# Top-k attention and two expert layers on one core: another order for the last tiles' expert stages

## The chip, the core and the metric

One core of a Trainium2 chip runs the whole program once. Five engines work side by side, each through its own list of instructions in order: TensorE (PE in the rows, with its weight loads as PEld), VectorE (DVE), ScalarE (ACT), GpSimd (POOL) and SyncE (SP), which here issues most DMAs. ACT's list issues some DMAs as well. The metric is device microseconds of one execution; the median of the runs shown counts.

## The reference

```python
scores = scale * q @ k.T                    # 2 batches, 8 heads, 576 rows, head_dim 64
kth    = the 32nd largest score of a row
attn   = softmax of the scores >= kth, all others out
x      = attn @ v                           # rows regrouped: 1152 tokens x 512
p = probs / (probs.sum(-1) + 1e-9)
out = sum over 4 experts e of p[:, e] * (relu(x @ w1[e]) @ w2[e])      # 512 -> 1024 -> 512
h = max(out @ m1, out @ m2, out @ m3)                                  # 512 -> 768
result = h @ mo                                                        # 768 -> 512
```

The second layer's matrices `m1`, `m2`, `m3` and `mo` arrive in float64, all else in float32.

## The kernel before

**Tiles and stages.** The 1152 tokens are 9 tiles of 128. Attention makes one tile after another, four head pairs each (36 pairs); its top-k runs on DVE as a chain of MAX8 and MATCH_REPLACE8. The expert layer is cut in two halves of experts (indices 0 to 3 and 4 to 7 of half-experts, `HALVES`), and a tile needs both. `STAGES` lists which tiles each stage works on; stages take the two halves in turn. Stage 0 is tile 0 alone with the first half, stages 1 to 6 are [0,1], [1,2] ... [5,6], so that each tile gets its second half in one stage and its first in the next or the other way round. Stage 7 is [6,7,8], stage 8 is [7,8]. After them come three passes of the second layer (`largest`), over three tiles each.

**Units.** A stage uses 16 weight units of 128 x 1024 (512 KB): for each of 4 half-experts two of the first layer ("a") and two of the second ("b"). SP loads a unit into one of four `raw` buffers (`w_load_to`), and `w_split_to` splits it: ACT rounds it to `whi`, then POOL subtracts to get `wlo`, in two halves of 128 x 512. From the first unit of stage `LATE` = 8 on, every other unit's subtraction is one DVE instruction of 128 x 1024 instead. Five pairs `hi`, `lo` are kept.

**Split products.** x lies split in a ring of four tiles (`xring`, xh and xl). `product` makes three matmuls for one: xl by whi, xh by whi, xh by wlo. In a first layer the 128 x 128 weight block stands and the tokens of all the stage's tiles move: 256 columns for two tiles, 384 for three. In a second layer the hidden values stand, tile by tile, and 512 columns of weights move. The hidden values are split as well: ACT makes `h` (or `hh`) with the ReLU, DVE subtracts for `hl`, every fourth time POOL.

**Float32.** Stage 0 isn't split. It multiplies whole float32 weights by `xfull`, tile 0 in float32. In the trace each such matmul has two records.

**The float64 matrices.** When attention has ended, `to_float32` narrows them in 48 pieces (`wide_load`, then two ACT, three DVE and one POOL instruction, then a DMA from ACT's list back to DRAM, from where `w_load_to` fetches them for `largest`). A new piece starts every second step of the loop, so up to three are under way. A piece's result lies in half of a `pt0` or `pt1` tile: four places, taken in turn. The first instruction of a piece, on ACT, writes there, so it waits until the DMA that emptied the place has landed.

**Order.** Nothing is scheduled at run time. A loop over attention's steps writes attention's instructions, and a counter of DVE time (`clock`) decides how many pieces of products are written in between. Each engine's list is fixed by that.

Of the kernel before, what the change touches and what calls it, by code (L numbers as in the profile page):

```python
# [27 lines left out]
WAITING = 2  # L28
S1 = 4
PAUSE = 0.8  # L30
LATE = 8
ON_POOL = ((0, 1, 2, 3, 4, 5, 6, 7), (0, 1, 2, 4, 5, 6))
W_AHEAD = 4
WIDE, W_FROM, W_STEP = 4, 306, 2
# [22 lines left out]
def kernel(  # L57
# [36 lines left out]
    def place(t):  # L94
        return (t - 1) % RING

    STAGES = [[0]] + [[t - 1, t] for t in range(1, NTILE - 2)] + [[NTILE - 3, NTILE - 2, NTILE - 1], [NTILE - 2, NTILE - 1]]
    STAGES = [sorted(x, key=place) for x in STAGES]
    HALVES = [range(E) if not n % 2 else range(E, 2 * E) for n in range(len(STAGES))]
    FIRST_IN = {t: min(n for n, x in enumerate(STAGES) if t in x) for t in range(NTILE)}  # L100
    LAST_IN = {t: max(n for n, x in enumerate(STAGES) if t in x) for t in range(NTILE)}
    assert all(set(x for n in range(len(STAGES)) if t in STAGES[n] for x in HALVES[n]) == set(range(2 * E)) for t in range(NTILE))
# [29 lines left out]
    def bank(name):  # L132
        return pg.tile([P, 512], F32, tag="g", name=name)
# [57 lines left out]
    order = list(w_units())  # L191
    w_index = {key: i for i, (key, _) in enumerate(order)}
    w_raw, w_hl = {}, {}
    w_pos = {"load": 0, "split": 0}

    def w_load_to(n):
        while w_pos["load"] < min(n, len(order)):
            key, src = order[w_pos["load"]]
            if key[1] in "cd" and narrowed[0] < WIDE * (narrow_at[key[2:]] + 1):
                return  # L200
            raw = wp.tile([P, 1024], F32, tag="raw", bufs=4, name="raw")
            nc.sync.dma_start(out=raw, in_=src)
            w_raw[key] = raw
            w_pos["load"] += 1
# [9 lines left out]
    def to_float32(n):  # L214

        raw = wide_raw.pop(n).rearrange("p (n t) -> p n t", t=2)
        low, high = raw[:, :, 0], raw[:, :, 1]
        last, hf = low.bitcast(I32), high.bitcast(F32)  # L220
        if not n % 2:
            narrow_to[0] = at.tile([P, NR, P], F32, tag="pt%d" % (n // 2 % 2), bufs=1, name="narrow").rearrange("p r n -> p (r n)")
        out = narrow_to[0][:, n % 2 * 256:n % 2 * 256 + 1024 // WIDE]
        t = out.bitcast(U32)
        nc.scalar.activation(out=out, in_=hf, func=AF.Abs)  # L225
        nc.scalar.activation(out=last, in_=low, func=AF.Copy, scale=2.0 ** -29)
        yield True
        nc.vector.scalar_tensor_tensor(out=hf, in0=out, scalar=LEAST, in1=hf, op0=ALU.is_ge, op1=ALU.mult)  # L228
        dve(1024 // WIDE)
        nc.vector.tensor_scalar(out=t, in0=high, scalar1=3, scalar2=0x3FFFFFF8, op0=ALU.logical_shift_left, op1=ALU.bitwise_and)  # L230
        dve(512 // WIDE)
        nc.vector.scalar_tensor_tensor(out=t, in0=high, scalar=0xC0000000, in1=t, op0=ALU.bitwise_and, op1=ALU.bitwise_or)  # L232
        dve(1024 // WIDE)
        yield True
        nc.gpsimd.tensor_tensor(out=out.bitcast(I32), in0=out.bitcast(I32), in1=last, op=ALU.add)  # L235
        yield True
        yield True
        wide_load(n + AHEAD_S)
        yield True
        nc.scalar.dma_start(out=narrow[wide[n // WIDE][0]][:, n % WIDE * 1024 // WIDE:(n % WIDE + 1) * 1024 // WIDE], in_=out)  # L240
        narrowed[0] = n + 1

    def w_split_to(n):
        while w_pos["split"] < min(n, len(order)):
            w_load_to(w_pos["split"] + 1)
            if w_pos["load"] == w_pos["split"]:
                return
            key, src = order[w_pos["split"]]
            raw = w_raw.pop(key)
            hi = wp.tile([P, 1024], F32R, tag="hi", name="whi")  # L250
            lo = wp.tile([P, 1024], F32R, tag="lo", name="wlo")
            nc.scalar.activation(out=hi, in_=raw, func=AF.Copy)  # L252

            late = w_pos["split"] - w_index[LATE, "a", HALVES[LATE][0], 0]
            on = nc.vector if late >= 0 and late % 2 else nc.gpsimd

            for x in (slice(0, 512), slice(512, 1024)) if on is nc.gpsimd else (slice(0, 1024),):
                on.tensor_tensor(out=lo[:, x], in0=raw[:, x], in1=hi[:, x].bitcast(F32), op=ALU.subtract)  # L258
            f = 512 if key[1] in "bd" else 256
            w_hl[key] = (hi.rearrange("p (a f) -> p a f", f=f), lo.rearrange("p (a f) -> p a f", f=f))  # L260
            w_pos["split"] += 1
            w_load_to(w_pos["split"] + 3)
# [107 lines left out]
    class Pair:  # L370
# [139 lines left out]

        def norm(self):
            assert "r" in self.did
            self.xt = xfull[:, self.hp, :] if not self.t else at.tile([P, P], F32, tag="xt", bufs=2 + WAITING, name="xt")
            nc.vector.tensor_tensor(out=self.xt, in0=self.x[:, 0:P], in1=self.r, op=ALU.mult)

        def split_x(self):
# [241 lines left out]
    def experts():  # L758
        begin = {}

        def half1(c, i, u):
            tiles = STAGES[c]
            N = len(tiles) * P
            for groups in layer1(weight((c, "a", i, u)), xs_of(tiles), N, begin.pop((c, i, u), None)):
                if groups is None:
                    tick()
                    yield True
            hh, hl = hidden(N)
            count = made_h[0] = made_h[0] + 1
            if ON_POOL_H and not count % ON_POOL_H:  # L770
                raw = ms.tile([P, 2 * WIDTH], F32, tag="tm", bufs=2, name="raw")
                later(lambda: [nc.scalar.activation(out=raw[:, g], in_=ps, func=AF.Relu) for g, ps in groups],
                      lambda: [nc.scalar.activation(out=hh[:, 0:2 * N], in_=raw[:, 0:2 * N], func=AF.Copy),  # L773
                               nc.gpsimd.tensor_tensor(out=hl[:, 0:2 * N], in0=raw[:, 0:2 * N], in1=hh[:, 0:2 * N].bitcast(F32), op=ALU.subtract),  # L774
                               made.add(("h", c, i, u))])
                yield hh, hl
                return
            dve(2 * N)
            later(lambda: [nc.scalar.activation(out=hh[:, g], in_=ps, func=AF.Relu) for g, ps in groups],
                  *[lambda: None] * H_LAG,  # L780
                  lambda: [nc.vector.scalar_tensor_tensor(out=hl[:, g], in0=ps, scalar=0.0, in1=hh[:, g].bitcast(F32),
                                                          op0=ALU.max, op1=ALU.subtract) for g, ps in groups]
                  + [made.add(("h", c, i, u))])
            yield hh, hl
# [3 lines left out]
        def half2(c, i, hs, ti):  # L788
# [2 lines left out]
                outs[t] = po.tile([P, DM], F32, tag="o", name="ps2") if ti < 2 else bank("ps2")  # L791
            ps = outs[t]
            assert {("h", c, i, 0), ("h", c, i, 1)} <= made
            yield from layer2(ps, [weight((c, "b", i, u), (c, "b", i, 0)) for u in range(2)], hs, len(STAGES[c]) * P, ti, not i % 2, i % 2 == 1)
            if not i % 2:
                return
            first = t not in accs
# [220 lines left out]
```

## Time and profile before

| | |
|---|---|
| times of three runs, us | 810.56, 812.18, 815.03 (median 812.18) |
| the profiled execution | 809.75 us, of it 808.0 us from the first to the last instruction |
| mean granted TensorE clock | 0.975 |
| PE busy | 746.8 us (92%) |
| DVE busy | 635.0 us (79%) |
| POOL busy | 552.7 us (68%) |
| ACT busy | 496.3 us (61%) |
| moved by DMA | 130.16 MB, 161 GB/s |

"Busy" is the time in which an engine's instructions run. PE's matmuls overlap, so 92% isn't the share of its peak: how much work a stretch holds is read from the distances between the starts of equal matmuls. The shares are means over very different stages.

### The profile page before, as it was taken

The page shows a single profiled execution, that of the slowest core. Times are in us where ns is not written, and L with a number is a line of the kernel's source. Part 1 is how long each engine was busy: PE and PEld are TensorE (multiplying, and loading weights), DVE is VectorE, ACT ScalarE, POOL GpSimd, SP SyncE. Part 2 cuts the span into 40 slices and gives each one's busy share as a digit, 9 for nine tenths or more (in the row PEclk, how much of TensorE's full clock was granted, in tenths as well). Part 3 has the DMA queues.
Part 4 walks back from the last instruction along what each step waited for, and adds up shares of the span by engine and source line. Part 5 has one row for each costly group of instructions (what it writes and reads, how often), then busy time and mean ns, then how long its engine had stood idle before and what let it go on. Part 6 is the DMA issues. An engine that isn't in the chain of part 4 may idle for free. (4 is left out here: it accounts for less than half of the span.)

```text
span 808.0 us, 13853 instructions
## 1 busy us (share of the span) xinstructions
PE 746.8 (92%) x4758; PEld 656.2 (81%) x4758; DVE 635.0 (79%) x1172; ACT 496.3 (61%) x1098; POOL 552.7 (68%) x467
## 2 busy tenths in 40 slices
PE   6879999999789999999999989889798689999998
PEld 3558688898679898898888978778687589899996
DVE  6999999988698989999999968977889754243341
ACT  4656868696677788788788755545446533433431
POOL 2648869887876787787868879987778653163420
PEclk9978999999899999999999999999989999999999
DMA  7663535635445444534543557776778553262511
GB/s 224 183 171 116 171 123 163 174 110 172 144 142 151 135 149 132 170 119 141 166 138 113 178 183 233 233 235 202 232 238 259 203 170 130 67 213 76 186 60 39
DMA packets 56054, 130.16 MB, mean 161 GB/s; under 512 B 9712, under 2 KB 23024, under 8 KB 55984
## 3 DMA queue, kind: packets, MB, share of 16 engines
q1 hardware_dynamic: 47632, 120.56, 48.0%
q10 hardware_dynamic: 8352, 8.72, 3.1%
q8 instruction: 37, 0.61, 0.3%
q14 instruction: 33, 0.27, 0.1%
HBM read 120.60 MB, written 8.65 MB: 160 GB/s over the span
## 5 line engine op out<-in xcount | busy, mean ns | idle before, releaser
L258 POOL TENSOR_TENSOR wlo<-raw,whi 128x512 fp32r<-128x512 f32 x274 | 367.2, 1369 | 134.8 <-ACT whi L252 134.7
L252 ACT ACTIVATE whi<-raw 128x1024 fp32r<-128x1024 f32 x164 | 169.5, 1058 | 33.3 <-POOL narrow L235 8.7
L649 PE MATMUL ps<-xl,whi 128*128 128x256 f32 (+1 forms) x584 | 174.0, 298 | 7.5 <-ACT pt L465 5.7
L650 PE MATMUL ps<-xh,whi 128*128 128x256 f32 (+1 forms) x584 | 171.8, 294 | 0.0
L651 PE MATMUL ps<-xh,wlo 128*128 128x256 f32 (+1 forms) x584 | 171.8, 294 | 0.0
L416 DVE MAX8 m<-work 128x8 f32<-128x576 f32 x216 | 154.8, 744 | 0.1
L649 PEld LDWEIGHTS ps<-xl,whi 128*128 128x128 f32 x584 | 110.8, 190 | 10.4 <-ACT pt L465 7.0
L650 PEld LDWEIGHTS ps<-xh,whi 128*128 128x128 f32 x584 | 110.8, 190 | 1.0
L651 PEld LDWEIGHTS ps<-xh,wlo 128*128 128x128 f32 x584 | 110.8, 190 | 0.0
L418 DVE MATCH_REPLACE8 work<-m,work 128x576 f32<-128x576 f32 x144 | 106.7, 741 | 0.0
L649 PE MATMUL ps<-wlo,h 128*128 128x512 f32 x224 | 91.0, 406 | 6.2 <-ACT h L773 3.3
L651 PE MATMUL ps<-whi,h 128*128 128x512 f32 x224 | 88.8, 396 | 5.8 <-POOL h L774 5.8
L650 PE MATMUL ps<-whi,h 128*128 128x512 f32 x224 | 88.6, 395 | 0.0
L258 DVE TENSOR_TENSOR wlo<-raw,whi 128x1024 fp32r<-128x1024 f32 x27 | 41.2, 1525 | 57.2 <-ACT whi L252 45.9
L225 ACT ACTIVATE narrow<-raw 128x256 f32<-128x256 f32 x48 | 20.8, 433 | 69.9 <-DMA narrow<-narrow 58.3
L235 POOL TENSOR_TENSOR narrow<-narrow,raw 128x256 int32<-128x256 int32 x48 | 44.3, 926 | 24.0 <-DVE narrow L232 8.3
L403 ACT ACTIVATE s<-pss 128x288 f32<-128x288 f32 x144 | 51.6, 408 | 14.4 <-PE pss L391 14.3
L651 PEld LDWEIGHTS ps<-whi,h 128*128 128x128 f32 x224 | 42.6, 190 | 17.0 <-POOL h L774 7.6
L416 DVE MAX8 m<-s 128x8 f32<-128x576 f32 x72 | 54.1, 751 | 2.8 <-ACT s L403 2.4
L649 PEld LDWEIGHTS ps<-wlo,h 128*128 128x128 f32 x224 | 42.8, 191 | 16.3 <-POOL wlo L258 5.5
L462 PE MATMUL psp<-ident,p 128*128 128x128 f32 x288 | 46.5, 287 | 9.6 <-POOL p L448 5.6
L649 PE MATMUL ps<-x2l,whi 128*128 128x384 f32 x144 | 49.4, 343 | 4.8 <-DVE x2l L853 4.8
(111 smaller groups left out, 1637.4 us busy)
## 6 DMA issues: line engine op xcount, KB each, us to landing
raw<-in_w_dram SPq DMA_DIRECT2D x128, 512.0 KB, 3.8
raw<-narrow SPq DMA_DIRECT2D x36, 512.0 KB, 3.3
raw<-in_m_dram SPq DMA_DIRECT2D x36, 256.0 KB, 4.0
whole<-in_w_dram SPq DMA_DIRECT2D x16, 512.0 KB, 5.9
narrow<-narrow ACTq DMA_DIRECT2D x48, 128.0 KB, 4.1
kraw<-in_k_dram SPq DMA_DIRECT2D x16, 288.0 KB, 4.5
qraw<-in_q_dram SPq DMA_DIRECT2D x48, 64.0 KB, 3.7
raw<-in_mo_dram SPq DMA_DIRECT2D x12, 256.0 KB, 4.7
```

What stands on the lines that cost most here:

```text
L225: nc.scalar.activation(out=out, in_=hf, func=AF.Abs)
L235: nc.gpsimd.tensor_tensor(out=out.bitcast(I32), in0=out.bitcast(I32), in1=last, op=ALU.add)
L252: nc.scalar.activation(out=hi, in_=raw, func=AF.Copy)
L258: on.tensor_tensor(out=lo[:, x], in0=raw[:, x], in1=hi[:, x].bitcast(F32), op=ALU.subtract)
L403: nc.scalar.activation(out=s[:, h, :], in_=halves[h][:, 0:SH], func=AF.Copy)
L416: nc.vector.max(m[:, 8 * r:8 * r + 8], src)
L418: nc.vector.match_replace(out=self.w[j], in_to_replace=m[:, 8 * r:8 * r + 8], in_values=src, imm_value=NEG)
L462: nc.tensor.transpose(ps[:, r * P:(r + 1) * P], self.p[:, part, part * TAIL + r * P:part * TAIL + (r + 1) * P], ident)
L649: nc.tensor.matmul(ps, lhsT=lh, rhs=rl, start=first, stop=False)
L650: nc.tensor.matmul(ps, lhsT=lh, rhs=rh, start=False, stop=False)
L651: nc.tensor.matmul(ps, lhsT=ll, rhs=rh, start=False, stop=last)
```

## The change

The stages become [0], [0,1], [1,2], [2,3], [3,4], [4,5], [5], [6,7,8], [6,7,8]. Stage 6, tile 5 with the first half of the experts, is computed in float32 as stage 0 is: `norm` writes tile 5's x to `xfull`, its 16 units aren't split but multiplied from `raw`, and no hidden value is split. Since those units keep their `raw` buffer until PE has used them, `w_load_to` gets a bound so that no load runs more than four units beyond the first one unused. Tile 6 moves from stage 6 to stage 8, which now has three tiles like stage 7. `LATE` goes from 8 to 7, so in stage 7 every other unit is subtracted on DVE, too. Converted pieces get eight places: even pieces take an `s1` tile (four of them, attention's before), odd ones take the four halves of `pt0` and `pt1`.

```diff
-LATE = 8
+LATE = 7
...
-    STAGES = [[0]] + [[t - 1, t] for t in range(1, NTILE - 2)] + [[NTILE - 3, NTILE - 2, NTILE - 1], [NTILE - 2, NTILE - 1]]
+    STAGES = [[0]] + [[t - 1, t] for t in range(1, NTILE - 3)] + [[NTILE - 4]] + [[NTILE - 3, NTILE - 2, NTILE - 1]] * 2
...
+    WHOLE = [n for n, x in enumerate(STAGES) if len(x) == 1]
...
+    whole_at = [i for i, (key, _) in enumerate(order) if key[0] in WHOLE and key[1] in "ab"]
...
+    used = [0]
+
     def w_load_to(n):
-        while w_pos["load"] < min(n, len(order)):
+        whole = [x for x in whole_at if x >= used[0]]
+        while w_pos["load"] < min(n, len(order), *[x + 4 for x in whole[:1]]):
...
         if not n % 2:
-            narrow_to[0] = at.tile([P, NR, P], F32, tag="pt%d" % (n // 2 % 2), bufs=1, name="narrow").rearrange("p r n -> p (r n)")
-        out = narrow_to[0][:, n % 2 * 256:n % 2 * 256 + 1024 // WIDE]
+            out = at.tile([P, 1024 // WIDE], F32, tag="s1", bufs=S1, name="narrow")
+        else:
+            if n % 4 == 1:
+                narrow_to[0] = at.tile([P, NR, P], F32, tag="pt%d" % (n // 4 % 2), bufs=1, name="narrow").rearrange("p r n -> p (r n)")
+            out = narrow_to[0][:, n // 2 % 2 * 256:n // 2 % 2 * 256 + 1024 // WIDE]
...
+            if key[0] in WHOLE and key[1] in "ab":
+                w_hl[key] = raw
+                w_pos["split"] += 1
+                w_load_to(w_pos["split"] + 3)
+                continue
...
-            self.xt = xfull[:, self.hp, :] if not self.t else at.tile([P, P], F32, tag="xt", bufs=2 + WAITING, name="xt")
+            self.xt = xfull[:, self.hp, :] if [self.t] in STAGES else at.tile([P, P], F32, tag="xt", bufs=2 + WAITING, name="xt")
...
+            if c in WHOLE:
+                ps = bank("ps1")
+                w = weight((c, "a", i, u)).rearrange("p (a f) -> p a f", f=256)
+                for f in range(2):
+                    for a in range(KT):
+                        pe(4 * P)
+                        nc.tensor.matmul(ps[:, f * P:(f + 1) * P], lhsT=w[:, a, f * P:(f + 1) * P], rhs=xfull[:, a, :], start=f == a == 0, stop=f == 1 and a == KT - 1)
+                    yield True
+                used[0] = w_index[c, "a", i, u] + 1
+                h = hp_.tile([P, 2, 512], F32, tag="h", bufs=4, name="hfull")[:, 0, 0:2 * P]
+                later(lambda: [nc.scalar.activation(out=h, in_=ps[:, 0:2 * P], func=AF.Relu), made.add(("h", c, i, u))])
+                yield h
+                return
...
-            yield from layer2(ps, [weight((c, "b", i, u), (c, "b", i, 0)) for u in range(2)], hs, len(STAGES[c]) * P, ti, not i % 2, i % 2 == 1)
+            if c in WHOLE:
+                for u in range(2):
+                    w = weight((c, "b", i, u), (c, "b", i, 0)).rearrange("p (f n) -> p f n", f=2)
+                    for f in range(2):
+                        pe(4 * DM)
+                        nc.tensor.matmul(ps, lhsT=hs[u][:, f * P:(f + 1) * P], rhs=w[:, f, :], start=not i % 2 and u == f == 0, stop=i % 2 == 1 and u == f == 1)
+                        yield True
+                used[0] = w_index[c, "b", i, 1] + 1
+            else:
+                yield from layer2(ps, [weight((c, "b", i, u), (c, "b", i, 0)) for u in range(2)], hs, len(STAGES[c]) * P, ti, not i % 2, i % 2 == 1)
```

What this does to the lists is seen in three places. The first is PE's list where stage 6 begins, behind the last matmuls of a second layer of stage 5. Before, with two tiles and split weights:

```order
L649 MATMUL ps_5753<-wlo,h 128x512
L650 MATMUL ps_5753<-whi,h 128x512
L651 MATMUL ps_5753<-whi,h 128x512
L649 MATMUL ps_5821<-xl,whi 128x256
L650 MATMUL ps_5821<-xh,whi 128x256
L651 MATMUL ps_5821<-xh,wlo 128x256
```

In the changed kernel, at the same place:

```order
L662 MATMUL ps_5737<-wlo,h 128x512
L663 MATMUL ps_5737<-whi,h 128x512
L664 MATMUL ps_5737<-whi,h 128x512
L783 MATMUL ps_5791<-xfull,raw 128x128 x8
L475 MATMUL psp<-ident,p 128x128 x4
L409 MATMUL pss<-kT,ql 128x288
```

A weight block's three matmuls of 256 columns have become one of 128 columns that reads the `raw` buffer itself.

The second place is SP's list around the first loads of float64 pieces (in_m_dram). Weight units are in_w_dram. Before:

```order
L304 DMA qraw<-in_q_dram 64x2x128 x2
L202 DMA raw<-in_w_dram 128x1024 x13
L212 DMA raw_6208<-in_m_dram 128x512
L212 DMA raw_6210<-in_m_dram 128x512
L212 DMA raw_6212<-in_m_dram 128x512
L212 DMA raw_6214<-in_m_dram 128x512
L212 DMA raw_6216<-in_m_dram 128x512
L202 DMA raw<-in_w_dram 128x1024 x2
L212 DMA raw_6272<-in_m_dram 128x512
```

In the changed kernel:

```order
L317 DMA qraw<-in_q_dram 64x2x128 x2
L207 DMA raw<-in_w_dram 128x1024 x10
L217 DMA raw_6082<-in_m_dram 128x512
L217 DMA raw_6084<-in_m_dram 128x512
L217 DMA raw_6086<-in_m_dram 128x512
L217 DMA raw_6088<-in_m_dram 128x512
L217 DMA raw_6090<-in_m_dram 128x512
L207 DMA raw<-in_w_dram 128x1024 x4
L217 DMA raw_6137<-in_m_dram 128x512
L217 DMA raw_6150<-in_m_dram 128x512
L207 DMA raw<-in_w_dram 128x1024 x3
```

Three unit loads fewer stand ahead of the five piece loads, and the four behind them belong to stage 6, which is then at its middle.

The third place is DVE's list where stage 7 begins, in the changed kernel (three instructions are one piece's):

```order
L728 SCALAR_TENSOR_TENSOR acc<-ps_6004,gate,acc 128x512
L271 TENSOR_TENSOR wlo<-raw,whi 128x1024
L236 SCALAR_TENSOR_TENSOR raw_6090<-narrow,raw_6090 128x256
L238 TENSOR_SCALAR narrow<-raw_6090 128x256
L240 SCALAR_TENSOR_TENSOR narrow<-raw_6090,narrow 128x256
L236 SCALAR_TENSOR_TENSOR raw_6137<-narrow,raw_6137 128x256
L238 TENSOR_SCALAR narrow<-raw_6137 128x256
```

Before, DVE's list holds pieces and hidden values there, and no weight unit:

```order
L715 SCALAR_TENSOR_TENSOR acc<-ps_6141,gate,acc 128x512
L228 SCALAR_TENSOR_TENSOR raw_6272<-narrow,raw_6272 128x256
L230 TENSOR_SCALAR narrow<-raw_6272 128x256
L232 SCALAR_TENSOR_TENSOR narrow<-raw_6272,narrow 128x256
L228 SCALAR_TENSOR_TENSOR raw_6332<-narrow,raw_6332 128x256
```

A unit's subtraction has come in between, ahead of the pieces that follow it in DVE's order.

## Rows read from the trace of the kernel before

**Rows 1.** The page: busy us of each engine, share of the span, instructions.

```profile
PE 746.8 (92%) x4758; PEld 656.2 (81%) x4758; DVE 635.0 (79%) x1172; ACT 496.3 (61%) x1098; POOL 552.7 (68%) x467
```

**Rows 2.** Busy time by stretches: length, then each engine (instructions), PE clock, DMA.

```profile
375.10:438.80 63.70, 62.67 (x470) 56.72 (x469) 60.81 (x130) 52.06 (x123) 50.41 (x44) 1.00 0.44 136
438.80:497.67 58.87, 54.80 (x381) 47.95 (x380) 50.08 (x82) 38.82 (x82) 49.79 (x42) 1.00 0.59 189
497.67:572.48 74.81, 67.00 (x325) 58.66 (x324) 61.32 (x76) 37.85 (x75) 64.67 (x56) 0.98 0.72 221
572.48:643.90 71.42, 60.79 (x337) 51.03 (x335) 58.73 (x78) 40.84 (x78) 50.71 (x39) 0.93 0.72 231
648.90:808.00 159.10, 155.49 (x834) 147.66 (x834) 55.96 (x73) 54.42 (x76) 54.96 (x38) 0.99 0.34 116
```

**Rows 3.** PE in order of time, where stages 7, 8 and the second layer begin.

```profile
497.67 0.34 PE L649 MATMUL ps<-xl,whi 128*128 128x384 f32 x1
...
498.71 0.34 PE L649 MATMUL ps<-xl,whi 128*128 128x384 f32 x1
...
569.68 0.40 PE L649 MATMUL ps<-wlo,hh 128*128 128x512 f32 x1
...
571.78 0.39 PE L649 MATMUL ps<-wlo,hh 128*128 128x512 f32 x1
...
572.48 0.28 PE L649 MATMUL ps<-xl,whi 128*128 128x256 f32 x1
...
573.90 0.28 PE L649 MATMUL ps<-xl,whi 128*128 128x256 f32 x1
...
648.90 0.52 PE L649 MATMUL ps<-x2l,whi 128*128 128x384 f32 x1 [4.79 <-DVE x2l L853]
```

**Rows 4.** PE in order of time in stage 0: float32, two records a matmul.

```profile
77.43 3.74 PE L733 MATMUL psa<-xfull,whole 128*128 128x128 f32 x32
...
87.47 2.74 PE L748 MATMUL ps<-whole,hfull 128*128 128x512 f32 x6
...
90.57 0.59 PE L748 MATMUL ps<-whole,hfull 128*128 128x512 f32 x1
```

**Rows 5.** What PE waited for between 497.67 and 643.9: us, times, longest.

```profile
PE ps L651 <- POOL h L774: 4.5, 3, 2.7
PE ps L651 <- POOL hl L774: 4.1, 2, 2.6
PE ps L649 <- POOL wlo L258: 3.5, 5, 1.2
PE ps L649 <- ACT h L773: 3.3, 1, 3.3
```

**Rows 6.** What ACT waited for in the same stretch.

```profile
ACT narrow L225 <- DMA narrow<-narrow: 54.4, 15, 7.7
ACT whi L252 <- POOL narrow L235: 8.7, 5, 2.2
```

**Rows 7.** Groups of instructions in the same stretch: busy us, mean ns, idle before.

```profile
L258 POOL TENSOR_TENSOR wlo<-raw,whi 128x512 fp32r<-128x512 f32 x51 | 72.7, 1450 | 7.2 <-ACT whi L252 7.2
...
L258 DVE TENSOR_TENSOR wlo<-raw,whi 128x1024 fp32r<-128x1024 f32 x10 | 16.3, 1633 | 4.9 <-ACT whi L252 4.9
```

**Rows 8.** A piece's instructions in the same stretch: ns least/median/most.

```profile
L230 DVE TENSOR_SCALAR narrow<-raw x39: 293/720/1721, 496.6 to 643.8; 128x256 uint32<-128x256 uint32 x39
...
L232 DVE SCALAR_TENSOR_TENSOR narrow<-raw,narrow x38: 424/851/1409, 497.9 to 636.6; 128x256 uint32<-128x256 uint32 x38
L228 DVE SCALAR_TENSOR_TENSOR raw<-narrow,raw x38: 407/828/1519, 499.8 to 642.2; 128x256 f32<-128x256 f32 x38
```

**Rows 9.** Loads from 438.8 to 497.67: KB each, median us to landing.

```profile
raw<-in_w_dram SPq DMA_DIRECT2D x14, 512.0 KB, 3.7
```

**Rows 10.** Loads from 30 to 70, around stage 0.

```profile
whole<-in_w_dram SPq DMA_DIRECT2D x8, 512.0 KB, 6.2
...
kraw<-in_k_dram SPq DMA_DIRECT2D x2, 288.0 KB, 7.6
```

## The prediction, made before the changed kernel had run

> **What bounds the kernel now.** I began with the page's busy times [rows 1]: PE is busy 92% of the span, the others 61 to 79%. That says PE counts most, not where it loses time. The stretches say that [rows 2]. In stage 5 (375.1 to 438.8) PE is busy for 62.67 of 63.70 us while DVE is at 60.81: attention and products fit together, and hardly anything is lost. In the second layer, from 648.90 on, PE is busy for 155.49 of 159.10. Between them lie stages 7 and 8 (497.67 to 643.9), where PE is busy for 67.00 of 74.81 and 60.79 of 71.42 and its clock falls to 0.98 and 0.93 on average. Attention is over there, and the float64 pieces are narrowed beside the products.
>
> How much is lost in those 146.2 us? PE's work is counted by the distance of starts [rows 3]. With 384 columns six matmuls take 498.71 − 497.67 = 1.04 us, so a weight block (three of them) takes 0.52. With 256 columns twelve take 1.42, so a block takes 0.355. In a second layer nine take 2.10, so three take 0.70. Stage 7 has 64 blocks of 0.52 (33.3) and 3 tiles x 16 x 0.70 (33.6). Stage 8 has 64 of 0.355 (22.7) and 2 x 16 x 0.70 (22.4). The last quarter of stage 6's second layer also stands there, 8 x 0.70 (5.6). Together 117.6, so **28.6 us** are not work. Named waits hold 15.4 of them, and each has ACT or POOL before it: hidden values and `wlo` that came late [rows 5]. The lower clock withholds up to 74.8 x 0.02 + 71.4 x 0.07 = 6.5.
>
> Why do ACT and POOL come late? ACT's waits answer it [rows 6]: 54.4 us in 15 waits of a piece's first instruction for the DMA that empties its place, and 8.7 behind POOL's part of a piece. ACT is busy for 37.85 + 40.84 = 78.7 [rows 2], so with these waits its list is full for 141.8 of the 146.2 us. Behind such a wait stand the ReLUs and the `whi` of the next unit; POOL's `wlo` waits for those, and PE for both.
>
> **The change part by part.** *Products.* In stage 0, float32 records start (3.74 − 0.28) / 31 = 0.112 us apart in the first layer, the tail of the last one taken like the 0.28 of a split record of 256 columns, and (2.74 − 0.59) / 5 = 0.43 in the second [rows 3, 4]. With two records a matmul, a block takes 0.223 in the first layer and 0.86 in the second. Stage 6's first layer becomes 64 x (0.223 − 0.355) = −8.4; stage 8's, now with three tiles, 64 x (0.52 − 0.355) = +10.6. In the second layer tile 5 costs 16 x (0.86 − 0.70) = +2.6, and tile 6 only moves. Sum **+4.7**, which PE pays in full, since nothing hides work on the engine that is busiest.
>
> *Eight places.* A place comes round every eighth piece in place of every fourth, and pieces start two steps apart, so the DMA that emptied it was issued seven steps earlier or more, not one. The 54.4 us of ACT's waits should nearly all go. What PE gets back is at most the 28.6, at least nothing, if another wait takes over. Next in line is DVE. From 497.67 to 643.9 it is busy for 61.32 + 58.73 = 120.1 [rows 2]. The third tile of stage 8 adds a little, and `LATE` = 7 adds eight subtractions of 1.63 in stage 7 [rows 7], some 13: about 133. PE's work from the start of stage 7 to the second layer will be 2 x (33.3 + 33.6) and 4 x 0.86 of stage 6's end, 137.2. The two are nearly level.
>
> DVE's own times can shrink. A piece's three instructions take 0.72 + 0.85 + 0.83 = 2.40 by their medians, but 0.29 + 0.42 + 0.41 = 1.12 at the least [rows 8]. POOL, busy for 64.67 + 50.71 = 115.4 us here [rows 2], does 51 half subtractions of 1.45 [rows 7]; 32 are left in the changed kernel, 27.6 us less. DVE at 133 keeps the waits, DVE at 133 − 39 x 1.28 = 83 has room. I take off a quarter of the difference, as POOL loses a quarter of its work: about 120 beside 137. On the Trainium skill, "GPSIMD Engine Reference", section Specifications: its SBUF interface is shared with VectorE, and contention arises with DVE instructions in a two-port mode or with two SBUF inputs. The spread from 293 to 1721 ns of one instruction is what this would look like. Taken alone the rule would let the pieces fall to their least times only with POOL idle, and put the eight subtractions moved to DVE into the same contention; by the least times the sum would be that of the first rival below, by the medians that of the second.
>
> So I let PE keep 11 of the 28.6 us, 8% of 137. Stage 5 shows that a DVE at 95% can leave PE less idle than that [rows 2], but a piece crosses ACT, DVE, POOL and ACT's list again, and any of these in-order lists can hold hidden values behind it. **−17.6**, bounds 0 and −28.6. The wait of 4.79 for x2l at the join to the second layer [rows 3] stays: it follows from the last tile's sum.
>
> *Stage 6 unsplit.* 16 x ACT and 32 x POOL instructions go. Much of that lies before 470 us, where PE and DVE set the pace together, so I count nothing for it, but it gave PE a cushion: five split pairs besides the four `raw` buffers. Now a buffer is loaded again only when PE has used it. A unit lasts PE 8 x 0.223 = 1.8 or 2 x 0.86 = 1.7 us, so from the release of a buffer to its next turn lie three units, 5.2 us. Loads land in 3.7 us around there [rows 9], and then nothing waits. The dense loads around stage 0 took 6.2 [rows 10], 1.0 more than the cushion, and 7.6 is the longest median there. With 16 units, four rounds, that is 0, 4 or 10 us. Stage 6 asks for 512 KB each 1.75 us beside the pieces, which is dense, so I take **+4**. While attention's matmuls still stand between, the cushion is longer. The two units of stage 7 that follow also have ACT and POOL to pass, which this has to cover.
>
> *Bookkeeping.* The bound in `w_load_to` is no instruction. Writing x to `xfull` in place of `xt` costs the same. Even pieces' `s1` tiles are free when attention is over, which is when pieces begin; if one were not, ACT would wait once for the last mask.
>
> Sum against the profiled span: 808.0 + 4.7 − 17.6 + 4 = 799.1, 8.9 less. From its 809.75 that gives 800.9. The median of the runs shown lies 2.4 above that execution, 812.18, so I predict 812.18 − 8.9 = **803**.
>
> **The rivals.** *More comes back.* DVE's times shrink toward their least, PE keeps 3 us as in a dense stage, and loads land in time: 808.0 + 4.7 − 25.6 = 787.1, so 791 by the median. For it: stage 5's packing. Against it: pieces cross four lists.
>
> *The wait changes its name.* ACT no longer waits for the DMA, but POOL's and DVE's parts of a piece are as late, DVE goes toward 133 of 137 and hidden values wait behind four pieces in its list. PE keeps 26: 808.0 + 4.7 − 2.6 + 4 = 814.1, so 818. For it: the 8.7 us that ACT already waits behind POOL's part [rows 6], and the order of DVE's list. Against it: POOL's quarter less. It decides from about 16 us kept besides the loads' 4 on: there the gain falls under 0.5%.
>
> *Slower: SP's list is held.* SP issues in order, and behind the five piece loads stand four unit loads of stage 6, behind the next two piece loads three, then one and four. Each piece load waits until POOL has finished an earlier piece. If three such holds last as long as the longest wait in a piece's chain, 7.7 us [rows 6], PE stands for 23 in stage 6: 808.0 + 4.7 − 17.6 + 23 = 818.1, so 822. It turns into a loss where holds pass (17.6 − 4.7) / 3 = 4.3 us. Against it: five pieces may be loaded ahead, and POOL has nothing to split then. On the Trainium skill, "DMA: Bandwidth & Descriptors", section "Issuing engines are not separate DMA queues": DMAs of all engines interleave on the same 16. By it, pieces that leave ACT's list sooner lengthen the landing of these very loads; the rise from 3.7 to 6.2 us agrees with such crowding, and no run here shows yet how far it goes.
>
> **How the numbers follow.** The forecast (797 to 809) gets 0.55, the first rival 0.17, the second 0.18, the third 0.10. About 0.5%, 4.1 us, is what a measurement can tell from no change: under 808.1 is faster, over 816.2 slower. Faster: 0.17 and 0.50 of the forecast's 0.55, 0.67. The second rival's values straddle the upper limit, so half of it is slower; with 0.08 of the third, slower is 0.17. The rest, 0.16, is the same. The range goes from 789, just below the first rival, to 818, the second, and leaves out mainly the third and the outer ends.
>
> **What would show it.** In the profile after: ACT's waits for DMA under a piece's first instruction nearly gone; stage 7's start to the second layer's about 148 us; its clock above 0.95. Stage 6's matmuls should have waits for in_w_dram of a few us in all. DVE in stages 7 and 8 near 120 to 125, its piece instructions with lower medians. I am wrong if ACT's waits go and PE's excess stays (then DVE or POOL releases it), if PE waits over 10 us for `raw` in stage 6, or if the last pieces arrive after stage 8 and hold the second layer's first units.

## The result, and the profile after

The changed kernel takes 790.1 us (median of four runs, 788.45 to 792.18) beside 811.37 for the kernel before in the same comparison: a ratio of 0.974, 95% interval 0.969 to 0.979. In two later comparisons it stood at 789.7 and 789.6 beside 809.7 and 809.9. The forecast was 803, range 789 to 818: the median lies 1.1 us inside the range's lower end. The profiled execution took 792.18 us, with a span of 790.3, 17.7 less than before. It is the slowest of the four, and the one of before was faster than its median, so the profiles show a little less than the medians. They are compared with each other below.

The page's line of busy times answers to [rows 1]:

```profile
PE 744.1 (94%) x4678; PEld 650.6 (82%) x4678; DVE 617.7 (78%) x1179; ACT 483.3 (61%) x1088; POOL 491.1 (62%) x419
```

PE has nearly the same busy time in a shorter span; POOL has lost 62 us. Where the span got shorter is seen from the stretches, cut at the same places as [rows 2]: stage 5, stage 6, stage 7, stage 8, second layer.

```profile
375.60:439.36 63.76, 62.73 (x469) 56.84 (x468) 61.13 (x132) 50.78 (x121) 45.49 (x40) 1.00 0.42 125
439.36:482.70 43.34, 39.72 (x270) 30.88 (x268) 29.19 (x63) 21.30 (x59) 11.22 (x12) 1.00 0.64 225
482.70:553.40 70.70, 65.23 (x310) 55.65 (x310) 56.07 (x80) 38.78 (x79) 45.12 (x37) 0.98 0.76 244
553.40:632.84 79.44, 77.36 (x385) 68.05 (x384) 74.50 (x109) 46.08 (x91) 59.23 (x48) 1.00 0.74 237
632.84:790.30 157.46, 153.87 (x835) 146.04 (x833) 53.65 (x68) 55.40 (x77) 52.17 (x37) 1.00 0.35 119
```

Stage 6 takes 43.34 us in place of 58.87, **15.5 less**. Stages 7 and 8 with the join take 150.14 in place of 151.23, **1.1 less**. The second layer takes 157.46 in place of 159.10, **1.6 less**. By the prediction's block times stage 6 has lost 8.4 + 12 x (1.40 − 0.86) = 14.9 us of work and stages 7 and 8 have gained 137.2 − 117.6 = 19.6. So stage 6 got shorter by its work and 0.6 us more, and stages 7 and 8 took in 19.6 us of work without getting longer. Their idle time, the join's 4.8 us included, fell from 33.6 to 12.9.

What PE and ACT waited for from 482.70 to 632.84 answers to [rows 5, 6] (us, times, longest):

```profile
PE ps L662 <- POOL wlo L271: 3.5, 1, 3.5
PE ps L664 <- POOL hl L800: 2.0, 2, 1.2
PE ps L664 <- POOL wlo L271: 1.6, 2, 0.8
```

```profile
ACT narrow L233 <- POOL narrow L243: 17.0, 10, 3.3
ACT whi L265 <- DMA raw<-in_w_dram: 11.7, 4, 5.3
ACT whi L265 <- POOL narrow L243: 11.2, 6, 3.0
```

The 54.4 us behind a piece's DMA are gone. In their place ACT stands 28 us behind POOL's part of a piece, which its list's DMAs wait for, and 11.7 for weight units, hardly there before (0.3 us).

A piece's DVE instructions in that stretch, beside [rows 8]:

```profile
L236 DVE SCALAR_TENSOR_TENSOR raw<-narrow,raw x44: 410/421/1039, 486.3 to 622.6; 128x256 f32<-128x256 f32 x44
L238 DVE TENSOR_SCALAR narrow<-raw x44: 293/725/1844, 487.3 to 623.1; 128x256 uint32<-128x256 uint32 x44
L240 DVE SCALAR_TENSOR_TENSOR narrow<-raw,narrow x44: 424/426/1495, 487.6 to 623.8; 128x256 uint32<-128x256 uint32 x44
```

Two of three medians are halved. By the means a piece's three instructions fell less, from 2.41 us together to 2.00, and 44 pieces lie in the stretch in place of 39. POOL is busy for 104 us there and not 115. The last piece's last DVE instruction starts at 623.8, nine us ahead of the join.

PE in order of time, stage 6 and the start of stage 7, then the join, answers to [rows 3, 4]:

```profile
465.97 3.74 PE L783 MATMUL ps<-xfull,raw 128*128 128x128 f32 x32
469.54 3.60 PE L825 MATMUL ps<-raw,hfull 128*128 128x512 f32 x8
...
475.74 2.05 PE L783 MATMUL ps<-xfull,raw 128*128 128x128 f32 x16 [0.82 <-DMA raw<-in_w_dram]
479.13 3.67 PE L825 MATMUL ps<-raw,hfull 128*128 128x512 f32 x8 [1.34 <-DMA raw<-in_w_dram]
...
484.09 0.44 PE L664 MATMUL ps<-xh,wlo 128*128 128x384 f32 x1 [0.79 <-POOL wlo L271]
...
632.84 0.34 PE L662 MATMUL ps<-x2l,whi 128*128 128x384 f32 x1
633.02 0.34 PE L663 MATMUL ps<-x2h,whi 128*128 128x384 f32 x1
```

The float32 rows have exactly stage 0's length (3.74 for 32 records; (3.60 − 0.59) / 7 = 0.43). Stage 6 waits for loads twice, 2.2 us in all, and stage 7 begins with a late `wlo`. The join has no wait. Stage 6's unit loads, from 439.4 to 482.7, beside [rows 9] with 3.7 us:

```profile
raw<-in_w_dram SPq DMA_DIRECT2D x14, 512.0 KB, 5.4
```

### The profile page after: what moved, and what is told of

Read it like the earlier page. It is cut to its first block, busy times and chain, and to the rows that moved or that the text cites. A ratio compares the mean times of both kernels' runs of the same rounds, so it can differ in the third digit from the quotient of the medians.

```text
span 790.3 us, 13610 instructions
## 1 busy us (share of the span) xinstructions
PE 744.1 (94%) x4678; PEld 650.6 (82%) x4678; DVE 617.7 (78%) x1179; ACT 483.3 (61%) x1088; POOL 491.1 (62%) x419
## 4 chain that ended last, share of the span: by engine, by line
PE 55%; POOL 9%; issue 7%; DVE 6%; ACT 5%; DMA 3%; ACTq 0%; SPq 0%; POOLq 0%; DVEq 0%
PE ps L662 13%; PE ps L664 13%; PE ps L663 13%; POOL wlo L271 6%; PE psv L520 3%; DMA raw<-in_w_dram 3%; PE pss L409 2%; ACT whi L265 2%; PE pso L664 2%; PE pso L663 2%; PE pso L662 2%; PE psp L475 2%; DVE m L429 1%; PE ps L783 1%; POOL narrow L243 1%
## 5 line engine op out<-in xcount | busy, mean ns | idle before, releaser
L271 POOL TENSOR_TENSOR wlo<-raw,whi 128x512 fp32r<-128x512 f32 x228 | 302.5, 1356 | 151.9 <-ACT whi L265 151.6
L265 ACT ACTIVATE whi<-raw 128x1024 fp32r<-128x1024 f32 x148 | 153.6, 1060 | 60.8 <-DMA raw<-in_w_dram 24.5
L662 PE MATMUL ps<-xl,whi 128*128 128x256 f32 (+1 forms) x520 | 159.5, 307 | 5.5 <-ACT pt L478 5.1
L664 PE MATMUL ps<-xh,wlo 128*128 128x256 f32 (+1 forms) x520 | 157.9, 304 | 1.6 <-POOL wlo L271 1.6
L663 PE MATMUL ps<-xh,whi 128*128 128x256 f32 (+1 forms) x520 | 157.6, 303 | 0.0
L662 PE MATMUL ps<-wlo,h 128*128 128x512 f32 x160 | 64.5, 403 | 0.6 <-POOL wlo L271 0.6
L664 PE MATMUL ps<-whi,h 128*128 128x512 f32 x160 | 62.8, 392 | 0.5 <-POOL h L800 0.5
L663 PE MATMUL ps<-whi,h 128*128 128x512 f32 x160 | 63.1, 394 | 0.0
L431 DVE MATCH_REPLACE8 work<-m,s 128x576 f32<-128x576 f32 x72 | 53.2, 739 | 0.0
L475 PEld LDWEIGHTS psp<-ident,p 128*128 128x128 f32 x288 | 35.2, 146 | 19.1 <-POOL p L461 6.9
L664 PE MATMUL ps<-x2h,wlo 128*128 128x384 f32 x144 | 48.7, 338 | 0.0
```

The source lines that it names most:

```text
L431: nc.vector.match_replace(out=self.w[j], in_to_replace=m[:, 8 * r:8 * r + 8], in_values=src, imm_value=NEG)
L475: nc.tensor.transpose(ps[:, r * P:(r + 1) * P], self.p[:, part, part * TAIL + r * P:part * TAIL + (r + 1) * P], ident)
L662: nc.tensor.matmul(ps, lhsT=lh, rhs=rl, start=first, stop=False)
L663: nc.tensor.matmul(ps, lhsT=lh, rhs=rh, start=False, stop=False)
L664: nc.tensor.matmul(ps, lhsT=ll, rhs=rh, start=False, stop=last)
```

## The experiments

At first I held that the eight places had given nearly all: ACT's waits are what they remove. The rival was the new order of stages with the unsplit stage 6. The first four kernels take the change apart.

**Eight places alone.** The kernel before, with this part of the diff only:

```diff
-            narrow_to[0] = at.tile([P, NR, P], F32, tag="pt%d" % (n // 2 % 2), bufs=1, name="narrow").rearrange("p r n -> p (r n)")
-        out = narrow_to[0][:, n % 2 * 256:n % 2 * 256 + 1024 // WIDE]
+            out = at.tile([P, 1024 // WIDE], F32, tag="s1", bufs=S1, name="narrow")
+        else:
+            if n % 4 == 1:
+                narrow_to[0] = at.tile([P, NR, P], F32, tag="pt%d" % (n // 4 % 2), bufs=1, name="narrow").rearrange("p r n -> p (r n)")
+            out = narrow_to[0][:, n // 2 % 2 * 256:n // 2 % 2 * 256 + 1024 // WIDE]
```

> The kernel before with eight places for converted pieces and nothing else. Theory (ACT standing for the DMA of a piece is what idles PE in stages 7 and 8 and at the join to the second layer): ACT's 54.4 us of waits for that DMA fall under 5, the stretch from stage 7's start to the second layer falls from 151 to 125 to 133 us, the join's 4.8 us go, and the time falls by 18 to 25 us against the kernel before, as far as or a little further than the whole change. Rival (the places matter only with the relief that the unsplit stage 6 gives POOL and ACT): the waits go, but POOL or DVE takes over and the time falls by under 9 us.

Measured: 797.6 beside 809.7 us, ratio 0.985 (0.983 to 0.988), 12 us less. The stretches, from stage 6 to the second layer (the same columns as above), and what PE and ACT waited for in the second and third:

```profile
439.30:498.20 58.90, 54.77 (x381) 47.93 (x380) 52.47 (x83) 39.80 (x84) 49.92 (x42) 1.00 0.61 190
498.20:570.60 72.40, 66.64 (x325) 58.94 (x325) 67.45 (x78) 39.01 (x77) 65.25 (x56) 0.98 0.77 235
570.60:639.20 68.60, 56.45 (x338) 48.03 (x336) 66.12 (x84) 41.23 (x77) 55.08 (x43) 0.98 0.78 252
```

```profile
PE ps L652 <- DVE x2l L856: 6.2, 1, 6.2
PE ps L654 <- POOL h L777: 4.8, 3, 2.7
```

```profile
ACT whi L255 <- POOL narrow L238: 13.4, 6, 5.7
ACT narrow L228 <- POOL narrow L238: 12.7, 7, 2.9
```

No wait for a piece's DMA is left, and still stages 7 and 8 take 141.0 us for 117.6 of work. DVE is busy for 67.45 + 66.12 = 133.6 of them, POOL for 120.3. The wait has changed its name, and neither theory's numbers fit: more than 9 us came, but not 18.

**Four places in the changed kernel**, the same edit the other way:

> The changed kernel with four places for converted pieces as before. Theory: the waits of ACT for the DMA come back (40 to 60 us) and with them PE's idle time; the time is 15 to 25 us above the changed kernel, thus -3 to +5 us against the kernel before (the 4.7 us of more PE work are then paid for nothing). Rival (relief by the unsplit stage and the new order make the gain): 3 to 9 us above the changed kernel, still 10 or more below the kernel before.

Measured: 796.6 beside 809.7 us, 0.985 (0.981 to 0.988), 13 us less than before and some 7 more than the changed kernel. ACT waits again:

```profile
ACT narrow L230 <- DMA narrow<-narrow: 48.3, 17, 7.2
```

```profile
436.70:479.70 43.00, 39.76 (x270) 30.88 (x268) 29.24 (x63) 21.29 (x59) 11.16 (x12) 1.00 0.65 227
479.70:550.40 70.70, 65.45 (x309) 54.17 (x309) 52.33 (x80) 37.02 (x75) 43.99 (x37) 1.00 0.75 242
550.40:634.70 84.30, 77.98 (x385) 67.95 (x384) 73.95 (x109) 47.15 (x95) 57.94 (x48) 1.00 0.71 223
```

My theory falls here. With ACT's waits nearly as long as ever, stages 7 and 8 take 155.0 us, 3.8 more than before, though they hold 19.6 more of PE's work, and stage 6 is 15.9 shorter. PE had been idle there for 33.6 us, and the work that the new order moves in fills that time. Without the eight places, the new order with float32 in stage 6 and `LATE` = 7 gives 13 us; the places alone give 12, and all together 20 to 21, less than the sum. I read that as both drawing on the same idle time. What the order gives without float32 and `LATE` = 7 is looked at further below.

**LATE = 8 in the changed kernel:**

> The changed kernel with LATE = 8, so that stage 7's subtractions are all on POOL again. Theory (PE bounds, neither DVE nor POOL is near its limit once ACT is free): within 3 us of the changed kernel; POOL busy in stage 7 rises by about 20 us, DVE falls by about 13. Rival one (DVE is next to PE): 3 us or more faster. Rival two (POOL is next): 5 us or more slower, with waits of PE for wlo.

Measured: 792.2 us, 0.979 (0.976 to 0.981), within noise of the changed kernel, as the theory had it. Its numbers for the engines didn't come: in the 150.6 us from stage 7's start to the second layer, DVE did 10 subtractions in place of 17 and was busy for more, 137.14 us beside 130.6, and POOL for 118.40. The 44 pieces take it: by the means, a piece's three DVE instructions took 2.41 us and not 2.00.

```profile
481.90:632.50 150.60, 143.18 (x693) 123.82 (x693) 137.14 (x181) 84.92 (x170) 118.40 (x99) 0.99 0.75 239
```

**Stage 6 split**, in the changed kernel:

```diff
-    WHOLE = [n for n, x in enumerate(STAGES) if len(x) == 1]
+    WHOLE = []
```

> The changed kernel with stage 6 (tile 5 alone) computed with split weights and split x as other stages are. Theory (leaving the split out is what makes a stage of one tile possible, because 16 units of 2.7 us on POOL don't fit beside one tile's matmuls): PE's work falls in the second layer by 16 x 0.16 = 2.6 us, but stage 6 grows from 43 to 48 us or more with PE waiting for wlo, and the time is 3 to 12 us above the changed kernel. Rival (only PE's work counts): 0 to 5 us below the changed kernel.

Measured: 788.1 beside 809.7 us, 0.973 (0.971 to 0.976). The theory falls: the split stage isn't held by POOL, and leaving the split out gained nothing. The stretches are stage 6, then 7 and 8. Below them, three of its matmuls of 128 columns follow each other in stage 6.

```profile
437.20:484.30 47.10, 45.03 (x345) 40.04 (x344) 32.19 (x65) 33.58 (x71) 41.16 (x36) 1.00 0.59 184
484.30:627.40 143.10, 138.98 (x697) 123.61 (x696) 137.16 (x189) 85.06 (x171) 105.51 (x86) 1.00 0.81 255
```

```profile
463.77 0.28 PE L663 MATMUL ps<-xh,whi 128*128 128x128 f32 x1
463.88 0.27 PE L664 MATMUL ps<-xh,wlo 128*128 128x128 f32 x1
463.99 0.28 PE L662 MATMUL ps<-xl,whi 128*128 128x128 f32 x1
```

A split matmul of 128 columns starts each 0.11 us, hardly faster than one of 256 (0.118), so a block costs 0.333 beside 0.223 in float32. Stage 6 thus has 64 x 0.11 = 7.0 more and 16 x 0.16 = 2.6 less work, part of it in stage 7. But stages 7 and 8 take 143.1 for 136.6 of work: 6.5 idle, not 12.9. What they don't have is the changed kernel's start of stage 7. Its waits of ACT from 478 to 515:

```profile
ACT whi L265 <- DMA raw<-in_w_dram: 21.2, 4, 10.4
```

With stage 6 split, the same waits from 480 to 517 come to 5.9 us. SP's list in the changed kernel, and what it waited for from 439.36 to 515, show why the units of stage 7 come late:

```profile
477.83 0.33 SPq L207 DMA_DIRECT2D raw<-in_w_dram  x1
487.01 0.33 SPq L217 DMA_DIRECT2D raw<-in_m_dram  x1
487.44 2.07 SPq L207 DMA_DIRECT2D raw<-in_w_dram  x4
```

```profile
SPq L207 <- PE ps L783: 19.8, 6, 8.7
SPq L217 <- POOL narrow L243: 16.5, 4, 8.8
```

The load at 477.83 had to wait until PE had used an unsplit unit. ACT's `whi` of the unit starts at 481.57, POOL's `wlo` follows, and behind it in POOL's list stands a part of a piece, which ends at 486.98. The piece load at 487.01 waits for that part, and four unit loads stand behind it in SP's list. So one late unit makes the next ones late. In all, float32 gives PE some 4.4 us of work less and takes back about as much in late units.

**Pieces without their work on DVE and POOL.** To see which of the two limits, ACT's DMA waits or the engines' work, binds at which point, these leave out a piece's three DVE instructions and the one on POOL; the lists stay in order otherwise. The first is the kernel before, the second the kernel before with eight places.

```diff
-        nc.vector.scalar_tensor_tensor(out=hf, in0=out, scalar=LEAST, in1=hf, op0=ALU.is_ge, op1=ALU.mult)
...
-        nc.vector.tensor_scalar(out=t, in0=high, scalar1=3, scalar2=0x3FFFFFF8, op0=ALU.logical_shift_left, op1=ALU.bitwise_and)
...
-        nc.vector.scalar_tensor_tensor(out=t, in0=high, scalar=0xC0000000, in1=t, op0=ALU.bitwise_and, op1=ALU.bitwise_or)
...
-        nc.gpsimd.tensor_tensor(out=out.bitcast(I32), in0=out.bitcast(I32), in1=last, op=ALU.add)
```

> The kernel before, four places, but a piece has only its two ACT instructions and its DMAs: the three DVE instructions and the one on POOL are left out, so the narrowed values are not those of the reference. Theory (ACT standing for the DMA binds stages 7 and 8 there): ACT's waits for the DMA of a piece stay over 30 us and the stretch from stage 7's start to the second layer, 151 us, falls only to 130 to 142. Rival (the work of the pieces on DVE and POOL binds): it falls to 118 to 128, near PE's 117.6.

> The kernel before with eight places and the same cheap pieces (DVE and POOL parts left out). With eight places and whole pieces the stretch took 140.9 us with DVE busy for 133.7 of it. Theory (with the DMA waits gone DVE and POOL bound the stretch, so the eight places alone could give back only ten of its 33.6 idle us): it falls to 118 to 124, PE's 117.6 and little more. Rival (something else, loads of units or the join, holds PE): it stays over 132.

Measured: 781.6 and 772.0 beside 809.7 us, 0.968 (0.964 to 0.972) and 0.953 (0.951 to 0.956). From stage 7's start to the second layer, with four places and its longest wait of ACT, then with eight:

```profile
496.20:630.70 134.50, 124.24 (x661) 108.79 (x660) 33.74 (x43) 77.99 (x153) 78.40 (x56) 0.96 0.76 246
```

```profile
ACT narrow L225 <- DMA narrow<-narrow: 51.3, 15, 8.1
```

```profile
494.30:612.80 118.50, 118.39 (x661) 106.50 (x659) 31.99 (x42) 77.30 (x149) 69.19 (x54) 1.00 0.84 277
```

In the profiles both expectations held: with DVE nearly free, ACT's waits for the DMA stay with four places, and the stretch is 16 us longer than with eight. But the profiled execution with four places is the slowest of its four, 789.95 us, 8.4 above the median. By the medians four places cost 9.6 us, so in a median execution the stretch may well have been under 130, where the rival had it; this wasn't measured. With eight, PE is busy for 118.39 of 118.50 us, and the block times' 117.6 are confirmed to a per cent. The four stretches are 151.2 us before, 141.0 with eight places, 134.5 with cheap pieces, 118.5 with both. By the medians of the whole kernel, eight places give 12.1 us with whole pieces and 9.6 with cheap ones, and cheap pieces 28.1 with four places and 25.6 with eight. So two causes hold PE up, each shown by taking it away, and their costs nearly add. Which of DVE and POOL makes the second isn't separated here, since cheap pieces relieve both.

**One step later for a piece's DMA**, in the kernel with stage 6 split and in the changed kernel:

```diff
+        yield True
         nc.scalar.dma_start(out=narrow[wide[n // WIDE][0]][:, n % WIDE * 1024 // WIDE:(n % WIDE + 1) * 1024 // WIDE], in_=out)
```

> The changed kernel once more, so that the split stage 6 and the next kernels stand beside it on one chip: 20 to 22 us below the kernel before.

> The changed kernel with stage 6 split, and with each piece's DMA issued one step later in ACT's list (eight places leave room for it). Theory (what ACT still waits for, 24.6 us behind POOL's part of a piece, stands in front of that DMA and delays the next unit's whi): these waits fall to under 12 us, PE's idle time in stages 7 and 8 falls by 1 to 4 us, and the time is 1 to 5 us below the kernel with stage 6 split. Rival (DVE, busy for 137 of 143 us there, sets the pace of that stretch): waits only change their name, the time stays within 1 us.

> The changed kernel with each piece's DMA issued one step later in ACT's list. Theory: ACT's 28 us of waits behind POOL's part of a piece fall by half, and as DVE (130 of 150 us) and POOL have room in this kernel, PE's idle time in stages 7 and 8 falls by 1 to 4 us and so does the time. Rival: these waits lie beside PE's work; within 1 us.

Measured: 786.7 us (0.973, 0.970 to 0.976) with the changed kernel at 789.7 (0.975, 0.973 to 0.978) beside it, and 788.7 (0.971, 0.967 to 0.976) with the changed kernel at 789.6. The intervals overlap widely, and no gain is shown. In the changed kernel with the later DMA, stages 7 and 8 took 147.3 us in the profile, beside 148.5 and 150.1 in two profiles of the changed kernel, and ACT's waits behind POOL's part of a piece came to 23 us: they didn't fall by half.

**Split stage 6 again, and with LATE = 8:**

> The changed kernel, to stand beside the next three on one chip: 19 to 22 us below the kernel before.

> The changed kernel with stage 6 split, once more, now beside the changed kernel itself. If leaving out the split is worth its 2.6 us of second-layer work and more, as the theory had it, this one is slower; the first run says 0 to 3 us faster. It should not be distinguishable from the changed kernel by more than 3 us.

> The changed kernel with stage 6 split and LATE = 8, so that all of stage 7's subtractions are on POOL. With stage 6 split DVE was busy for 137 of the 143 us of stages 7 and 8. If DVE sets the pace there, taking eight subtractions of 1.2 to 1.6 us from it gives 2 to 6 us back. If DVE's instructions stretch with POOL's work instead, as with LATE = 8 alone, where DVE's busy time rose by 6 us, the time stays or rises by up to 3 us.

Measured: 789.6 for the changed kernel (0.974, 0.970 to 0.978), 790.5 with stage 6 split (0.974, 0.970 to 0.978) and 798.1 with LATE = 8 as well (0.983, 0.979 to 0.988). Splitting stage 6 or not shows no difference. LATE = 7 matters once stage 6 is split, about 7 us, against what "DVE sets the pace" would say and more than the other reading allowed (3 us). Stage 7 in the kernel with LATE = 8, then in the one with LATE = 7:

```profile
483.50:554.30 70.80, 64.86 (x314) 56.44 (x313) 62.45 (x74) 38.41 (x76) 65.98 (x56) 0.98 0.75 240
```

```profile
486.30:549.90 63.60, 61.85 (x313) 55.62 (x312) 62.33 (x79) 37.75 (x74) 49.09 (x39) 1.00 0.79 259
```

With LATE = 8 all subtractions of stage 7 are on POOL (65.98 us beside 49.09). DVE has five instructions fewer, is busy for as long (62.45 beside 62.33), and the stage takes 7 us more. With LATE = 8 this is the fastest of six executions, 791.95 us, so its profile shows less than the medians do.

This last kernel is also the kernel with eight places alone and the new order besides. By the medians it gains nothing on that one (0.983 beside 0.985). So with eight places the order was seen to pay only together with `LATE` = 7 (790.5) or with float32 in stage 6 (792.2). With four places the order was not run by itself, and the 13 us above belong to the three together.

No version was shown to beat the changed kernel.

## Why the prediction was right, and where its sizes were off

The direction and the places held, and so did the range, but only just: 790.1 lies 1.1 us above its lower end, one execution (788.45) below it, and the band given most weight, 797 to 809, was missed. The gain was 17.7 us in the profiles and 21.3 by the medians, beside 8.9 forecast. That so large a miss stayed inside the range is luck: had the late units below cost the forecast 4 us and not 6.4, the same kernel would have come to 787.7. Point by point:

- **What bounds it.** Right: PE's work counted by starts came out as measured with cheap pieces and eight places (118.5 for 117.6), and most of the lost time lay in stages 7 and 8.
- **Products, +4.7.** Right in size: float32 has stage 0's distances, and the stretches move by −14.9 and +19.6 us of work. "PE pays in full, since nothing hides work on the engine that is busiest" was wrong as a reading. The 19.6 us went to stretches in which PE stood idle: with four places they lengthened them by 3.8 only. I had put the whole gain down to the places and a cost to the order; the places alone give 12 us, and the order with float32 and `LATE` = 7 gives 13.
- **Eight places, −17.6.** The waits went, as said. That a place's worth is bounded by the next engine in line was right, and in the kernel with eight places alone it was the second rival's picture: DVE busy for 133.6 of 141.0 us. With the order as well, I let PE keep 11 us. That made the stretch 148 us long, which leaves out the join's 4.8 that I had kept besides; it took 150.1 without a join. PE kept 12.9, and about half of that belongs to the next term: without late units, in the kernel with stage 6 split, 6.5 were left. DVE was busy for 130.6 us, not 120, though its pieces' medians fell to 1.57 us from 2.40. Medians were the wrong measure: the means fell to 2.00 from 2.41, and there were 44 pieces and not 39. Nor did POOL lose the quarter that this step stood on: it went from 115.4 us to 104.4, since 36 half subtractions were left and not 32 (50.5 us beside 72.7) and its part of the pieces grew (45 for 46.9 us beside 39 for 37.2).
- **Stage 6's loads, +4.** Right in kind, placed wrong. Stage 6 itself waited 2.2 us for units, and made it up elsewhere. The bill comes in stage 7's first units, 12.9 − 6.5 = 6.4 us. PE's waits for late weights there are 5.5 us in four waits, beside 1.8 with stage 6 split. Loads landed in 5.4 us, near the cushion of 5.2 and between the 3.7 and 6.2 that I had. I had said that unsplitting costs the cushion, but not that it gains nothing on balance.
- **The join, 4.79 us.** This step failed: "it follows from the last tile's sum". The wait is gone. DVE's list of the kernel before shows why:

```profile
644.42 0.75 DVE L853 TENSOR_TENSOR x2l<-pst,x2h 128x384 fp32r<-128x384 f32 x2
645.09 0.52 DVE L228 SCALAR_TENSOR_TENSOR raw<-narrow,raw 128x256 f32<-128x256 f32 x1
645.70 1.18 DVE L230 TENSOR_SCALAR narrow<-raw 128x256 uint32<-128x256 uint32 x1
646.91 1.38 DVE L232 SCALAR_TENSOR_TENSOR narrow<-raw,narrow 128x256 uint32<-128x256 uint32 x1
648.21 0.74 DVE L853 TENSOR_TENSOR x2l<-pst,x2h 128x384 fp32r<-128x384 f32 x2
```

The x2l that PE waited for stood behind one of the last pieces, though ACT had made its x2h by 641.3. In the changed kernel pieces end before stage 8 does. With eight places alone they don't, and the wait was 6.2 us there. With four places and the new order it is gone as well. So it is the longer stage 8, not the places, that covers it.
- **The second layer, 0.** It got 1.6 us shorter. After the join's idle time the kernel before goes on at the slow clock, below: 0.50 for 1.7 us and 0.63 for the next 2.1, which withholds 1.6.

The sum with measured terms: +4.7, idle time in stages 7 and 8 from 28.6 to 6.5 (−22.1), late units +6.4, stage 6 −0.6, join −4.8, second layer −1.6, start of stage 6 +0.6: −17.4 of the profiles' −17.7. Mis-sized were mainly the two terms at the join (0 against −6.4) and the idle time kept (11 against 6.5); the late units (4 against 6.4) worked the other way.

Of the rivals, "more comes back" gave the right time, 791, by luck: DVE's pieces did shrink, but PE kept 12.9 us and not 3, loads were late, and the join, which this rival left alone, made up for it. "SP's list is held" came in small and in another place: behind POOL's part of a piece SP's list stood for 0.7 us in stage 6 and three times, 15.8 us in all, at the start of stage 7. PE met that as late `whi` and `wlo`, within the 5.5 us above and not as 23; no wait of PE for a load itself was over 1.34 us. On the Trainium skill's rule of the shared SBUF interface ("GPSIMD Engine Reference", section Specifications), the run with LATE = 8 and stage 6 in float32 agrees: DVE with seven subtractions fewer in the stretch was busy for 137.14 us beside 130.6, while POOL's time rose from 104 to 118.40.

What stays open is how much of the changed kernel's last 12.9 us could go; the later DMA didn't settle it.

## What to carry to other kernels

When an engine waits in a stretch that another list paces, there are two ways to use it: shorten that list, or move work of the idle engine there. They draw on the same idle time, so price them together and not one as gain and the other as cost. Run the parts by themselves, too: here the order paid only with another part beside it. After removing a wait, read the next busiest list of the same stretch first. The wait's length (54 us) said little: 10 us of the stretch came back. The next list's busy time is no fixed bound either: DVE was busy for 125.0 of 151.3 us before and for 133.7 of 141.1 with eight places, doing the same work, as its instructions got longer. And compare a profiled execution with its median before taking a difference of two profiles for the effect. And look for a wait at a stage's join in the list of the engine that releases it; what stands ahead there may have nothing to do with the stage.

## What the runs showed of the hardware

A split matmul of 128 columns started each 0.11 us and one of 256 each 0.118, so halving the columns gave 6% and not half.

DVE's instructions took longer where POOL was busy for more of the stretch. A piece's three together took by their means 1.94 us with POOL busy for 66% of stages 7 and 8 (four places in the changed kernel), 2.00 with 70% (the changed kernel), 2.16 with 74% (stage 6 split), 2.41 with 79% (before, and LATE = 8), 2.43 with 82% (LATE = 8 and stage 6 split) and 2.70 with 85% (eight places alone). The order is the same throughout; no run set POOL's share by itself.

And idle time costs twice: after 4.79 us without work the kernel before starts its second layer with a granted clock of 0.50, the lower of TensorE's two levels (1.2 GHz), and with 0.32 us between matmuls that start each 0.175 in the changed kernel, where no idle time came before and the clock stood at 1.00. The kernel before, the stretch after the join and its first matmuls there:

```profile
649.20:650.90 1.70, 1.70 (x7) 1.70 (x7) 1.70 (x3) 0.00 (x0) 1.70 (x2) 0.50 0.68 272
```

```profile
649.22 0.52 PE L650 MATMUL ps<-x2h,whi 128*128 128x384 f32 x1
649.54 0.52 PE L651 MATMUL ps<-x2h,wlo 128*128 128x384 f32 x1
```
